# The bonus term of the first twelve attention cells as two-column matmuls, and another order of the first operations

## The chip, the cores and the metric

The kernel runs on one core of a Trainium2 chip. The metric is the device time of one execution in microseconds, the median of several executions. A core has five engines that run their own instruction streams: PE (TensorE, matmul; PEld is its loading of weights), DVE (VectorE), ACT (ScalarE), POOL (GpSimd) and SP (SyncE, which here issues nearly all DMA transfers).

## The reference

Three layers follow one another: a linear attention with a decaying state and a bonus `u` for the present token, a mixture of 4 experts that is computed densely, and an MLP with `h * cos(h)`.

```python
# attention: batch 4, heads 8, sequence 768, head size 48
for t in range(S):
    kt, vt, rt = (k[:, :, t], v[:, :, t], r[:, :, t])
    cur = np.einsum('bhd,bhe->bhde', u[None] * kt, vt)
    y[:, :, t] = np.einsum('bhd,bhde->bhe', rt, state + cur)
    state = w[None, :, :, None] * state + np.einsum('bhd,bhe->bhde', kt, vt)
# experts: N = 3072 tokens, D = 384, E = 4, F = 1024
for e in range(E):
    h = np.maximum(x @ w1[e], 0.0)
    out += p[:, e:e + 1] * (h @ w2[e])
# MLP: 384 -> 2048 -> 384
h = x @ w_in
out = (h * np.cos(h)) @ w_out
```

The bonus of a token is one number per head, `sum over d of r*u*k`, times the value row `v` of that token.

## The kernel before

**Attention** is cut into 24 cells `c`, each of 128 tokens (two chunks of 64) of one batch element with all 8 heads in 4 pairs. The first four cells begin the four batch elements. A cell loads `t` (tile `rkt`: r and k with channels in the partitions, heads in pairs) and `tok` (tile `tok`: r, k, v with tokens in the partitions). Its steps, in the names that the order tables show:

- `a_r` and `a_kt` scale r and k in `rkt` by powers of the decay (128x512 products, on DVE and POOL). The product of scaled r and scaled k at one token holds one surplus factor 1/w per channel.
- `a_ru`, `a_rk`, `a_sum`, `a_dv` make the bonus from `tok`: r times u (POOL, 128x384), times k (DVE, 128x384), a sum over d (DVE, into `dsum`), and that times v (POOL, in place in `tok[:, 0:2]`).
- `a_kp` (DVE) scales k for the state. `a_score0` and `a_state0` (later both in `a_first`) are 16 matmuls of 64x64 and 16 of 64x48, `a_mask` (DVE) masks the scores into `s`, `a_state` (ACT, DVE) and `a_state2` (three POOL products) carry the state on.
- `a_in` (16 matmuls of `s` by v) and `a_out` (8 or 16 matmuls of the state by r) sum into one PSUM bank, and the last operation of `a_out` adds the bonus and writes `yo` (DVE).
- `a_x` transposes `yo` on PE into the bank `px`; `split` writes a high part `xh` (ACT) and a low part `xl` (DVE), the inputs of the experts' matmuls.

Cells 0 and 1 of the kernel before have the bonus in another way: `l_ru` (ACT, 4 small products a cell) makes r times u, `l_bonus_pe` makes a second set of 16 score matmuls of it, `l_mask(c, 1)` keeps their diagonal (DVE), and a second run of `a_in` adds them.

**Experts and MLP** are a list of items. An item is 9 matmuls up (`hp`) and 9 down (`a`), each with weights of 128x128 and 512 moving columns (256 in the first items), in fp32r with high and low parts: three products for each pair. Weight blocks arrive by DMA in tile `s` and `w_split` makes high and low parts of them (`w`: ACT, then DVE or POOL).

**Order.** Every engine runs its instructions in the order of the program, which is written by hand. The first operations stand line by line in the last part of the function: set-up, cells 0 and 1, and `a_r`, `a_kt` for cell 2. Then the loop over items begins. A table `offsets` gives each step of cell c a place `6 * c + offset`; sorted by it, the steps are dealt out between the matmuls of the items (`mix`), the PE steps so many per item, the others as they come. SP issues DMA in program order too; a transfer waits there for its buffer and for an earlier transfer of the same slot.

Of the kernel before, what the change touches and what calls it, by code (L numbers as in the profile page):

```python
# [26 lines left out]
def attention_moe_cos_mlp_kernel(  # L27
# [61 lines left out]

    HD = HP * D  # L90
    ONE_GROUP = 4
    mask = at_p.tile([128, 2, C], F32, name="mask")
    wk_tok = at_p.tile([128, 2, HP, D], F32, name="wk_tok")
    u_tok = at_p.tile([128, 2, HP, D], F32, name="u_tok")
    pw = at_p.tile([128, HP, 129], F32, name="pw")
# [3 lines left out]
    sw = [at_p.tile([128, HP, D], F32, name=f"sw{b}") for b in range(B)]  # L99

    kps = [at_p.tile([128, 2 * HD + 16], F32, name=f"kp{x}") for x in range(2)]
    cells = [(b, i) for i in range(NCH) for b in range(B)]
    yd = {}
    pair_ps = ps_p.tile([128, 2, 512], F32, name="pair_ps")
# [103 lines left out]
                    )  # L208


    def l_load(c):
        b, i = cells[c]
        t = ld_p.tile([128, 8, HP, D], F32, tag="tok", name="tok")
        nc.sync.dma_start(out=t[:, 2:8].rearrange("q x p d -> q (x p d)"), in_=tok_in[b, i][:, 2 * HD:])
        ld[c]["tok"] = t

    def l_ru(c, ps):
        if "ru" not in ld[c]:
            ld[c]["ru"] = acc[2].rearrange("q b d -> q (b d)")[:, c * 512:c * 512 + 512].rearrange("q (p t) -> q p t", p=HP)
        for p in ps:  # L220
            nc.scalar.activation(out=ld[c]["ru"][:, p, :], in_=ld[c]["t"][:, 0, p, :], func=ACTF.Copy, scale=wpair[:, 1, p:p + 1])

    def l_bonus_pe(c):
        a_score_pe(c, False, ld[c]["ru"], ld[c]["ps_s"])

    def l_mask(c, x):
        ps = ld[c]["ps_s" if x else "ps"]
        s_ = t_p.tile([128, 2, HP, C], F32, tag="s", name="s")
        nc.vector.tensor_tensor(
            out=s_.rearrange("q c p t -> q c (p t)").rearrange("q c (p t) -> q c p t", t=C),  # L230
            in0=ps[:, :, HD:HD + HP * C].rearrange("q c (p t) -> q c p t", t=C),
            in1=mask[:, x].unsqueeze(1).unsqueeze(1).to_broadcast([128, 2, HP, C]),
            op=ALU.mult,
        )
        ld[c]["s"] = s_
# [32 lines left out]
    def a_mask(c):  # L268
        ps = ld[c]["ps"]
        s_ = t_p.tile([128, 2, HP, C], F32, tag="s", name="s")  # L270
        nc.vector.tensor_tensor(
            out=s_.rearrange("q c p t -> q c (p t)").rearrange("q c (p t) -> q c p t", t=C),
            in0=ps[:, :, HD:HD + HP * C].rearrange("q c (p t) -> q c p t", t=C),
            in1=mask[:, 0].unsqueeze(1).unsqueeze(1).to_broadcast([128, 2, HP, C]),
            op=ALU.mult,
        )
        ld[c]["s"] = s_
# [28 lines left out]
    def a_out(c):  # L306
        b, i = cells[c]
        d = ld[c]
        tok, t, ps = d["tok"], d["t"], d["ps_y"]
        apart = c >= ONE_GROUP  # L310
        if apart:
            a_in(c)
        for p in range(HP):
            for ch in range(2):
                if i == 0 and ch == 0:
                    continue
                for par in range(2):
# [11 lines left out]
        y4, p4 = yo.rearrange("q (p a d) -> q a p d", a=2, d=D), ps[:, :, 0:HD].rearrange("q a (p d) -> q a p d", d=D)  # L329
        if "ru" in d:  # L330
            nc.scalar.activation(out=y4, in_=p4, func=ACTF.Copy)
        else:
            nc.vector.tensor_tensor(out=y4, in0=p4, in1=tok[:, 0:2], op=ALU.add)
# [12 lines left out]

    def a_x(c):
        b, i = cells[c]
        if i < PASS_TB:
            px = x_bank()[:, 0:DM].rearrange("q (k t) -> q k t", k=KD)  # L350
            for kk in range(KD):
                nc.tensor.transpose(px[:, kk, :], ld[c]["yo"][:, kk * 128:kk * 128 + 128], ident)
            split(xh[i][:, :, b * 128:b * 128 + 128], xl[i][:, :, b * 128:b * 128 + 128], px)
        ld.pop(c)
# [10 lines left out]
    def a_one(c):  # L365
# [3 lines left out]
            a_first(c)  # L369

    offsets = [
        (a_load_t, -15), (a_load_tok, -15.5), (a_ru, -9), (a_r, -5.6), (a_rk, -5.5), (a_kt, -4), (a_kp, -2.6), (a_sum, -2.5), (a_dv, -2.4),
        (a_one, 0), (a_in, 2.4), (a_out, 3), (a_state2, 3.2),
    ]
    on_pe = (a_one, a_in, a_out, a_x)
    steps = sorted((6 * c + o, c, k_) for c in range(NC_ + 1) for k_, (f, o) in enumerate(offsets) if (c < NC_ or f == a_one) and not (f == a_in and c >= ONE_GROUP))
    ahead = {(f, c) for f, _ in offsets for c in range(2)}
    ahead |= {(f, 2) for f in (a_load_t, a_load_tok, a_r, a_ru, a_kt)} | {(a_load_t, 3), (a_load_tok, 3)}
    steps = [(offsets[k_][0], c) for key, c, k_ in steps if (offsets[k_][0], c) not in ahead]


# [238 lines left out]
    def warm(n):  # L620
# [3 lines left out]
        for _ in range(n):  # L624
            nc.tensor.matmul(hp, wu_a, wu_b, start=True, stop=True)

    wpair = at_p.tile([128, 3, HP], F32, name="wpair")
    tk = at_p.tile([128, HP, 2, C], F32, name="tk")

    def setup():  # L630
        nc.sync.dma_start(out=wpair[:, 0:2].rearrange("q a p -> q (a p)"), in_=w_pair)
        a_load_t(0)
        l_load(0)
        a_load_t(1)
        prob_load()
# [9 lines left out]
        for x, op in enumerate((ALU.is_gt, ALU.is_equal)):  # L645
            for o in (0, 64):
                nc.gpsimd.affine_select(
                    out=mask[o:o + 64, x], in_=mask[o:o + 64, x], pattern=[[1, C]], base=0, channel_multiplier=-1,
                    compare_op=op, fill=0.0,
                )  # L650


    def powers():
# [15 lines left out]
        nc.gpsimd.tensor_tensor(out=uw, in0=uw, in1=wp, op=ALU.mult)  # L669
        n = 1  # L670
        while n < 96:
            k_ = min(n, 96 - n)
# [104 lines left out]
    with tc.manual_schedule():  # L777
# [2 lines left out]
        setup()  # L780
        warm(14)
        powers()
        w_loads(1)
        a_load_t(2)
        nc.sync.dma_start(out=u_tok.rearrange("q a p d -> q (a p d)"), in_=u_rep)
        a_load_tok(2)
        w_loads(3)
        a_r(0)
        a_kt(0, nc.vector)
        l_ru(0, (0, 1))  # L790
        table()
        l_ru(0, (2, 3))
        a_score0(0)
        a_kp(0)
        a_state0(0)
        a_kt(1)
        l_mask(0, 0)
        l_bonus_pe(0)
        a_in(0, True, False)
        l_mask(0, 1)  # L800
# [11 lines left out]
        a_load_t(3)
        a_load_tok(3)
        w_loads(4)
        a_in(1, True, False)
        l_mask(1, 1)
        a_x(0)
        a_state(1)
        a_in(1, False)
        prob_norm()  # L820
        prob_store()
        warm(1)
        a_out(1)
        a_state2(0)
        a_r(2)
        a_kt(2)
        a_ru(2)
        w_splits(2)
# [309 lines left out]
```

## Time and profile before

| | |
|---|---|
| median of 3 executions | 1284.65 us (1284.12 to 1285.16) |
| profiled execution | 1283.49 us |
| its span, first to last instruction | 1281.4 us |
| PE busy | 1263.5 us (99%) |
| DVE, ACT, POOL busy | 758.7, 472.8, 219.4 us |
| mean granted clock of PE | 0.995 |
| PE busy in the first 22.20 us | 16.02 us |

The busy time of PE counts overlapping matmuls once, and says little on how dense they are. That is read from the starts of successive matmuls. A line of the timeline holds start, length, engine, source line, operation, output <- inputs, shape, count, and in brackets the idle time before it with what ended it. "issue" means that nothing in the trace explains the wait.

### The profile page before, as it was taken

The numbers are of one execution on the slowest core, as the hardware profiler recorded it, in microseconds if no ns is written. First come the engines' busy times: TensorE is split into PE (matmuls) and PEld (weight loads), VectorE is DVE, ScalarE is ACT, GpSimd is POOL, SyncE is SP. The second block draws the span as 40 slices with busy tenths as digits, with TensorE's granted clock in tenths as the row PEclk, the third lists the DMA queues.
The fourth block names the chain that finished last, engine by engine and source line by source line (L and its number), as shares of the span: only waits on it lengthen the run. The fifth ranks groups of instructions, "written<-read, shape, count | busy, mean of one in ns | idle before, by whom it ended". The sixth has DMA issues, their size and how long they took to land.

```text
span 1281.4 us, 20582 instructions
## 1 busy us (share of the span) xinstructions
PE 1263.5 (99%) x8516; PEld 1046.3 (82%) x8517; DVE 758.7 (59%) x1255; ACT 472.8 (37%) x826; POOL 219.4 (17%) x235
## 2 busy tenths in 40 slices
PE   7999999999999999999999999999999999999997
PEld 5888888888888888888888888888888888888886
DVE  6785675433233366556546557534777777777775
ACT  3221221121122222122122112114777777777774
POOL 5764554111111111000111111112001001001000
PEclk8999999999999999999999999999999999999999
DMA  7552464121013235234234134224005006006001
GB/s 277 186 209 89 174 225 151 40 70 34 21 58 119 74 119 169 75 103 144 60 112 149 58 96 130 62 109 153 2 17 181 25 27 198 23 1 188 18 18 51
DMA packets 54247, 128.72 MB, mean 100 GB/s; under 512 B 5025, under 2 KB 27522, under 8 KB 54146
## 3 DMA queue, kind: packets, MB, share of 16 engines
q1 hardware_dynamic: 49394, 102.03, 24.0%
q0 software_dynamic: 4608, 25.17, 6.2%
q8 instruction: 69, 1.13, 0.4%
q14 instruction: 32, 0.26, 0.1%
q10 hardware_dynamic: 144, 0.13, 0.0%
HBM read 105.24 MB, written 22.07 MB: 99 GB/s over the span
## 4 chain that ended last, share of the span: by engine, by line


## 5 line engine op out<-in xcount | busy, mean ns | idle before, releaser
L488 PE MATMUL hp<-xh,w 128*128 128x512 f32 (+1 forms) x888 | 347.4, 391 | 1.0 <-ACT xh L108 0.6
L489 PE MATMUL hp<-xl,w 128*128 128x512 f32 (+1 forms) x888 | 341.9, 385 | 1.5 <-DVE xl L109 1.5
L490 PE MATMUL hp<-xh,w 128*128 128x512 f32 (+1 forms) x888 | 341.8, 385 | 0.0
L556 PE MATMUL a<-gh,w 128*128 128x512 f32 (+1 forms) x880 | 338.4, 385 | 0.0
L558 PE MATMUL a<-gl,w 128*128 128x512 f32 (+1 forms) x880 | 337.7, 384 | 0.0
L557 PE MATMUL a<-gh,w 128*128 128x512 f32 (+1 forms) x880 | 337.7, 384 | 0.0
L497 ACT ACTIVATE gh<-hp 128x512 fp32r<-128x512 f32 (+1 forms) x200 | 116.2, 581 | 596.7 <-PE hp L490 583.7
L498 DVE SCALAR_TENSOR_TENSOR gl<-hp,gh 128x512 fp32r<-128x512 f32 (+1 forms) x200 | 133.1, 667 | 305.9 <-ACT gh L497 305.1
L488 PEld LDWEIGHTS hp<-xh,w 128*128 128x128 f32 x888 | 167.7, 189 | 35.2 <-ACT xh L108 0.8
L489 PEld LDWEIGHTS hp<-xl,w 128*128 128x128 f32 x888 | 167.9, 189 | 32.9 <-DVE xl L109 1.7
L490 PEld LDWEIGHTS hp<-xh,w 128*128 128x128 f32 x888 | 167.6, 189 | 33.1
L556 PEld LDWEIGHTS a<-gh,w 128*128 128x128 f32 x880 | 165.5, 188 | 33.2 <-ACT rr L515 0.4
L558 PEld LDWEIGHTS a<-gl,w 128*128 128x128 f32 x880 | 165.4, 188 | 32.6
L557 PEld LDWEIGHTS a<-gh,w 128*128 128x128 f32 x880 | 165.5, 188 | 32.2
L579 POOL TENSOR_TENSOR acc<-acc,pm 128x512 f32<-128x512 f32 x54 | 72.6, 1373 | 563.9 <-DVE pm L578 563.9
L517 DVE SCALAR_TENSOR_TENSOR hs<-rr,hs 128x512 f32<-128x512 f32 x96 | 67.4, 702 | 62.0 <-ACT rr L516 62.0
L509 DVE SCALAR_TENSOR_TENSOR rr<-ni,hs 128x512 f32<-128x512 int32 x96 | 66.3, 691 | 44.6 <-ACT ni L508 44.6
L515 ACT ACTIVATE rr<-rr 128x512 f32<-128x512 f32 x96 | 60.8, 633 | 86.0 <-DVE rr L510 86.0
L407 POOL DMA_DIRECT2D w<-dec x32 | 17.1, 536 | 300.3 <-PE a L558 299.5
L510 DVE SCALAR_TENSOR_TENSOR rr<-ni,rr 128x512 f32<-128x512 int32 x96 | 66.5, 693 | 3.3
L109 DVE TENSOR_TENSOR gl<-hs,gh 128x512 fp32r<-128x512 f32 x96 | 66.0, 688 | 0.7 <-ACT gh L108 0.7
L405 DVE TENSOR_TENSOR w<-s,w 128x768 fp32r<-128x768 f32 x60 | 63.6, 1059 | 1.7 <-ACT w L404 0.3
(122 smaller groups left out, 977.5 us busy)
## 6 DMA issues: line engine op xcount, KB each, us to landing
s<-in_moe_wb_dram SPq DMA_DIRECT2D x64, 384.0 KB, 3.7
w<-dec POOLq DMA_DIRECT2D x32, 768.0 KB, 4.5
tok<-in_tok_in_dram SPq DMA_DIRECT2D x22, 768.0 KB, 4.6
rkt<-in_rkt_dram SPq DMA_DIRECT2D x24, 512.0 KB, 6.1
draw<-in_moe_wb_dram SPq DMA_DIRECT2D x32, 384.0 KB, 3.8
dec<-dout SPq DMA_DIRECT2D x32, 384.0 KB, 3.0
pb<-pn SPq DMA_DIRECT2D x24, 256.0 KB, 5.0
out_dram<-acc SPq DMA_DIRECT2D x17, 256.0 KB, 2.1
```

The source lines that it names most:

```text
L488: nc.tensor.matmul(hp, wh[:, kk, :], x_h[:, kk, :], start=kk == 0, stop=False)
L489: nc.tensor.matmul(hp, wh[:, kk, :], x_l[:, kk, :], start=False, stop=False)
L490: nc.tensor.matmul(hp, wl[:, kk, :], x_h[:, kk, :], start=False, stop=kk == KD - 1)
L497: nc.scalar.activation(out=gh, in_=hp, func=ACTF.Relu)
L498: nc.vector.scalar_tensor_tensor(out=gl, in0=hp, scalar=0.0, in1=gh.bitcast(F32), op0=ALU.max, op1=ALU.subtract)
L509: nc.vector.scalar_tensor_tensor(out=rr, in0=ni, scalar=-PI2_HI, in1=hs, op0=ALU.mult, op1=ALU.add)
L510: nc.vector.scalar_tensor_tensor(out=rr, in0=ni, scalar=-PI2_LO, in1=rr, op0=ALU.mult, op1=ALU.add)
L517: nc.vector.scalar_tensor_tensor(out=hs, in0=rr, scalar=1.0, in1=hs, op0=ALU.subtract, op1=ALU.mult)
L556: nc.tensor.matmul(a, wh[:, ds], gh, start=q == 0, stop=False)
L557: nc.tensor.matmul(a, wl[:, ds], gh, start=False, stop=False)
L558: nc.tensor.matmul(a, wh[:, ds], gl, start=False, stop=q == BLK - 1)
L579: nc.gpsimd.tensor_tensor(out=o, in0=o, in1=m, op=ALU.add)
```

## The change

1. The bonus of cells 0 to 11 (`PRODS = 12`) no longer uses r of `tok`. `l_prod` (POOL) multiplies scaled r by scaled k in `rkt`, 128x512. `l_sum` sums over channels on PE: 4 matmuls, one per head pair, with the product (128x128) as weights and a moving operand of 2 columns, `uw2`, which holds u times w in the upper or lower 64 partitions. ACT copies the 8 results per token to `dsum`, and `a_dv` and the addition in `a_out` go on as before. `l_sum` writes to the bank `px`, which the transposes of `a_x` also use.
2. `a_ru`, `a_rk` and `a_sum` are gone for cells 2 to 11, and `l_ru`, `l_bonus_pe`, the second `l_mask` and the second half of `a_in` for cells 0 and 1. `l_load` leaves r out of `tok` for cells 2 to 11 as well (576 KB in place of 768 KB).
3. For cells 2 to 11 `l_sum` and `a_dv` stand at the head of `a_out`; before, `a_sum` and `a_dv` stood ahead of `a_first`. `a_kt` moves from offset -4 to -6.5.
4. The first operations stand in another order: the expert probabilities are loaded and normalised earlier, `a_out(0)` stands ahead of `a_state0(1)`, the transposes of both cells stand behind `a_out(1)`, `a_x(1)` goes to another bank, and `a_load_t(3)`, `l_load(3)` wait for `a_out(0)` as before, which comes earlier.

```diff
+    PRODS = 12
+    prods = [
+        acc[2].rearrange("q b d -> q (b d)")[:, x * 512:x * 512 + 512].rearrange("q (p t) -> q p t", p=HP) for x in range(2)
+    ]
...
+    def l_prod(c, eng=None):
+        o = prods[c % 2]
+        t = ld[c]["t"]
+        (eng or nc.gpsimd).tensor_tensor(out=o, in0=t[:, 0], in1=t[:, 1], op=ALU.mult)
+        ld[c]["prod"] = o
+
+    def l_sum(c):
+        ps = x_bank()[:, 0:2 * HP].rearrange("q (p a) -> q p a", a=2)
+        for p in range(HP):
+            nc.tensor.matmul(ps[:, p, :], ld[c]["prod"][:, p, :], uw2[:, p, :], start=p == 0, stop=True, skip_group_check=True)
+        ds = t_p.tile([128, 2, HP], F32, tag="dsum", name="dsum")
+        nc.scalar.activation(out=ds.rearrange("q a p -> q p a"), in_=ps, func=ACTF.Copy)
+        ld[c]["ds"] = ds
...
         apart = c >= ONE_GROUP
+        if 2 <= c < PRODS:
+            l_sum(c)
+            a_dv(c)
         if apart:
             a_in(c)
...
-            px = x_bank()[:, 0:DM].rearrange("q (k t) -> q k t", k=KD)
+            px = (pair_ps[:, 0] if c == 1 else x_bank())[:, 0:DM].rearrange("q (k t) -> q k t", k=KD)
...
     offsets = [
-        (a_load_t, -15), (a_load_tok, -15.5), (a_ru, -9), (a_r, -5.6), (a_rk, -5.5), (a_kt, -4), (a_kp, -2.6), (a_sum, -2.5), (a_dv, -2.4),
+        (a_load_t, -15), (l_load, -15.5), (a_load_tok, -15.5), (a_ru, -9), (a_kt, -6.5), (a_r, -5.6), (l_prod, -5.55), (a_rk, -5.5), (a_kp, -2.6), (a_sum, -2.5), (a_dv, -2.4),
         (a_one, 0), (a_in, 2.4), (a_out, 3), (a_state2, 3.2),
     ]
...
+        prob_norm()
         w_loads(1)
         a_load_t(2)
+        l_load(2)
+        w_loads(3)
         nc.sync.dma_start(out=u_tok.rearrange("q a p d -> q (a p d)"), in_=u_rep)
-        a_load_tok(2)
-        w_loads(3)
         a_r(0)
         a_kt(0, nc.vector)
-        l_ru(0, (0, 1))
+        prob_scale()
+        prob_store()
         table()
-        l_ru(0, (2, 3))
+        l_prod(0)
+        a_kt(1)
         a_score0(0)
         a_kp(0)
+        a_mask(0)
         a_state0(0)
...
```

The program's order on PE at its start, before: behind the set-up transposes (`px<-ident,tk`), cell 0 and cell 1 up to the first item's matmul (`hp`). `L203` are scores, `L189` the state, `L295` `a_in`, `L321` `a_out`, `L352` the transposes of `a_x`, `L625` warm-up matmuls.

```order
L203 MATMUL ds_ps<-acc_106,rkt 64x64 x16
L295 MATMUL dy_ps<-tok,s 64x48 x32
L203 MATMUL pair_ps<-rkt 64x64 x16
L189 MATMUL ds_ps<-tok,kp_128 64x48 x16
L321 MATMUL dy_ps<-st_1_112,rkt 64x48 x8
L203 MATMUL ds_ps<-acc_106,rkt 64x64 x16
L295 MATMUL dy_ps<-tok,s 64x48 x16
L352 MATMUL px<-ident,yo 128x128 x3
L295 MATMUL dy_ps<-tok,s 64x48 x16
```

The same place of the changed kernel, where `L207` are scores, `L193` the state, `L230` `l_sum`, `L293` `a_in`, `L322` `a_out`, `L354` the transposes:

```order
L230 MATMUL px<-uw_132,acc_106 128x2 x4
L293 MATMUL dy_ps<-tok,s 64x48 x16
L207 MATMUL pair_ps<-rkt 64x64 x16
L322 MATMUL dy_ps<-st_1_112,rkt 64x48 x8
L193 MATMUL ds_ps<-tok,kp_128 64x48 x16
L230 MATMUL px<-uw_132,acc_106 128x2 x4
L293 MATMUL dy_ps<-tok,s 64x48 x16
L322 MATMUL dy_ps<-st_1_115,rkt 64x48 x8
L354 MATMUL px<-ident,yo 128x128 x3
```

Two sets of 16 scores and two of 16 `a_in` matmuls are gone, two sets of 4 two-column matmuls are in, and `a_out(0)` stands ahead of the state of cell 1.

In the changed kernel PE has this at cell 4, behind the up matmuls of an item (`L490` to `L492`):

```order
L492 MATMUL hp<-xh_98,w 128x256
L230 MATMUL px<-uw_132,acc_106 128x2 x4
L293 MATMUL pair_ps<-tok,s 64x48 x16
L322 MATMUL pair_ps<-st_2_113,rkt 64x48 x2
L322 MATMUL pair_ps<-st_0_111,rkt 64x48 x2
```

The four matmuls of `l_sum` are new here; what follows them followed the up matmul `hp` directly. Cells 2 to 11 have this once each.

DVE between the end of cell 1 and the state of cell 2, before: `L109` is `xl`, `L405` a weight split, `L149` `a_rk`, `L158` `a_kp`, `L153` `a_sum`, `L137` `a_r`.

```order
L137 TENSOR_TENSOR rkt<-rkt,pw 128x512
L405 TENSOR_TENSOR w<-s,w 128x768
L109 TENSOR_TENSOR xl_101<-px,xh_98 128x3x128
L405 TENSOR_TENSOR w<-s,w 128x768
L149 TENSOR_TENSOR tok<-tok 128x384
L158 TENSOR_TENSOR kp_127<-tok,wk_tok 128x384
```

And in the changed kernel, where `L330` is the addition of the bonus into `yo`, `L141` `a_r`, `L113` `xl`, `L407` the weight split, `L162` `a_kp`:

```order
L330 TENSOR_TENSOR yo<-dy_ps,tok 128x2x4x48 x2
L141 TENSOR_TENSOR rkt<-rkt,pw 128x512
L113 TENSOR_TENSOR xl_101<-px,xh_98 128x3x128
L113 TENSOR_TENSOR xl_101<-pair_ps,xh_98 128x3x128
L407 TENSOR_TENSOR w<-s,w 128x768 x2
L162 TENSOR_TENSOR kp_127<-tok,wk_tok 128x384
```

`a_rk` is gone from this stretch, and the first weight split has moved behind the `xl` of cell 1.

## Rows read from the trace of the kernel before

**Rows 1.** Stretches: busy us (instructions) of PE, PEld, DVE, ACT, POOL; clock, DMA, GB/s:

```profile
0.00:22.20 22.20, 16.02 (x378) 10.93 (x380) 10.98 (x31) 9.64 (x25) 9.43 (x24) 0.92 0.79 286
22.20:60.00 37.80, 33.58 (x640) 30.65 (x641) 29.38 (x45) 11.17 (x26) 30.40 (x30) 0.91 0.60 201
600.00:800.00 200.00, 200.00 (x884) 165.74 (x883) 117.20 (x217) 41.07 (x65) 24.42 (x18) 1.00 0.32 100
```

**Rows 2.** Waits of PE over the whole span: us in total, times, longest:

```profile
PE ds_ps L189 <- issue: 2.9, 1, 2.9
PE pair_ps L189 <- DVE kp L158: 1.7, 1, 1.7
PE hp L489 <- DVE xl L109: 1.5, 1, 1.5
PE pair_ps L295 <- DVE st L252: 0.4, 1, 0.4
PE hp L488 <- DVE gl L498: 0.4, 1, 0.4
```

**Rows 3.** Timeline of PE and PEld around a cell's transposes and scores:

```profile
61.43 0.28 PE L489 MATMUL hp<-xl,w 128*128 128x256 f32 x1
61.44 0.19 PEld L490 LDWEIGHTS hp<-xh,w 128*128 128x128 f32 x1
61.55 0.28 PE L490 MATMUL hp<-xh,w 128*128 128x256 f32 x1
61.57 0.35 PEld L352 LDWEIGHTS px<-ident,yo 128*128 128x128 f32 x3
61.67 0.49 PE L352 MATMUL px<-ident,yo 128*128 128x128 f32 x3
...
62.09 0.69 PE L203 MATMUL pair_ps<-rkt 64*64 64x64 f32 x32
```

**Rows 4.** Timeline of PE in the first operations:

```profile
14.92 0.50 PE L189 MATMUL ds_ps<-tok,kp 64*64 64x48 f32 x20 [2.93 <-issue]
...
16.54 1.11 PE L295 MATMUL dy_ps<-tok,s 64*64 64x48 f32 x32
...
21.07 0.55 PE L352 MATMUL px<-ident,yo 128*128 128x128 f32 x3
...
26.95 1.11 PE L189 MATMUL pair_ps<-tok,kp 64*64 64x48 f32 x32 [1.74 <-DVE kp L158]
```

**Rows 5.** DMA queues from 12.0 to 12.5 us: packets, MB, share of 16 engines:

```profile
q1 hardware_dynamic: 33, 0.20, 98.0%
q8 instruction: 1, 0.02, 12.8%
```

**Rows 6.** Timeline of ACT and DVE between the transposes of cell 1 and the state of cell 2:

```profile
21.66 0.49 ACT L108 ACTIVATE xh<-px 128x384 fp32r<-128x384 f32 x1
...
22.04 0.83 ACT L404 ACTIVATE w<-s 128x768 fp32r<-128x768 f32 x1
...
23.95 1.28 DVE L405 TENSOR_TENSOR w<-s,w 128x768 fp32r<-128x768 f32 x1
...
25.16 0.86 DVE L149 TENSOR_TENSOR tok<-tok 128x384 f32<-128x384 f32 x1
...
25.94 0.95 DVE L158 TENSOR_TENSOR kp<-tok,wk_tok 128x384 f32<-128x384 f32 x1
```

**Rows 7.** Two of the stretches of 2 us, columns as in the first group:

```profile
16.00:18.00 2.00, 2.00 (x61) 1.89 (x50) 0.69 (x1) 1.22 (x2) 0.70 (x1) 0.50 0.45 113
...
30.00:32.00 2.00, 2.00 (x37) 1.71 (x36) 1.35 (x2) 1.02 (x3) 1.68 (x2) 0.50 0.59 236
32.00:34.00 2.00, 2.00 (x25) 1.81 (x24) 0.42 (x1) 1.08 (x2) 2.00 (x3) 0.74 0.22 25
```

**Rows 8.** Operations by form, over the span: busy us, mean ns, idle before:

```profile
L145 POOL TENSOR_TENSOR tok<-tok,u_tok 128x384 f32<-128x384 f32 x22 | 24.8, 1129 | 11.5 <-DMA tok<-in_tok_in_dram 11.4
L165 POOL TENSOR_TENSOR tok<-tok,dsum 128x384 f32<-128x384 f32 x22 | 18.3, 830 | 63.2 <-DVE dsum L153 63.2
```

More of the change, by code (lines that the diff above doesn't have):

```diff
@@ L91, in attention_moe_cos_mlp_kernel @@
     ONE_GROUP = 4
-    mask = at_p.tile([128, 2, C], F32, name="mask")
+    PRODS = 12
+    mask = at_p.tile([128, C], F32, name="mask")
     wk_tok = at_p.tile([128, 2, HP, D], F32, name="wk_tok")
@@ L208, in a_score_pe, with l_load @@
                     )
-    def l_load(c):
+    def l_load(c, eng=None):
         b, i = cells[c]
@@ L214, in l_load @@
         nc.sync.dma_start(out=t[:, 2:8].rearrange("q x p d -> q (x p d)"), in_=tok_in[b, i][:, 2 * HD:])
[L215 to L235, printed above, removed]
+        ld.setdefault(c, {})["tok"] = t
+    def l_prod(c, eng=None):
[10 more added lines that the diff above has]
+        ld[c]["ds"] = ds
     def a_state(c):
@@ L273, in a_mask @@
             in0=ps[:, :, HD:HD + HP * C].rearrange("q c (p t) -> q c p t", t=C),
-            in1=mask[:, 0].unsqueeze(1).unsqueeze(1).to_broadcast([128, 2, HP, C]),
+            in1=mask.unsqueeze(1).unsqueeze(1).to_broadcast([128, 2, HP, C]),
             op=ALU.mult,
@@ L328, in a_out @@
         d["yo"] = yo
[L329 to L333, printed above, removed]
+        nc.vector.tensor_tensor(
+            out=yo.rearrange("q (p a d) -> q a p d", a=2, d=D),
+            in0=ps[:, :, 0:HD].rearrange("q a (p d) -> q a p d", d=D),
+            in1=tok[:, 0:2],
+            op=ALU.add,
+        )
         if apart:
@@ L375, in attention_moe_cos_mlp_kernel @@
     on_pe = (a_one, a_in, a_out, a_x)
-    steps = sorted((6 * c + o, c, k_) for c in range(NC_ + 1) for k_, (f, o) in enumerate(offsets) if (c < NC_ or f == a_one) and not (f == a_in and c >= ONE_GROUP))
+    steps = sorted((6 * c + o, c, k_) for c in range(NC_ + 1) for k_, (f, o) in enumerate(offsets) if (c < NC_ or f == a_one) and not (f == a_in and c >= ONE_GROUP) and not (f in ((a_load_tok, a_ru, a_rk, a_sum, a_dv) if c < PRODS else (l_load, l_prod))))
     ahead = {(f, c) for f, _ in offsets for c in range(2)}
-    ahead |= {(f, 2) for f in (a_load_t, a_load_tok, a_r, a_ru, a_kt)} | {(a_load_t, 3), (a_load_tok, 3)}
+    ahead |= {(f, 2) for f in (a_load_t, l_load, a_r, l_prod, a_kt)} | {(a_load_t, 3), (l_load, 3)}
     steps = [(offsets[k_][0], c) for key, c, k_ in steps if (offsets[k_][0], c) not in ahead]
@@ L625, in warm @@
             nc.tensor.matmul(hp, wu_a, wu_b, start=True, stop=True)
+    uw2 = at_p.tile([128, HP, 2], F32, name="uw2")
     wpair = at_p.tile([128, 3, HP], F32, name="wpair")
@@ L631, in setup @@
         nc.sync.dma_start(out=wpair[:, 0:2].rearrange("q a p -> q (a p)"), in_=w_pair)
+        prob_load()
         a_load_t(0)
@@ L634, in setup @@
         a_load_t(1)
-        prob_load()
         l_load(1)
@@ L638, in setup @@
             nc.vector.memset(t[:, 2 * HD:], 0.0)
+        nc.gpsimd.memset(uw2, 0.0)
         nc.gpsimd.memset(ident, 1.0)
@@ L644, in setup @@
         nc.gpsimd.memset(mask, 1.0)
[L645 to L650, printed above, removed]
+        for o in (0, 64):
+            nc.gpsimd.affine_select(
+                out=mask[o:o + 64], in_=mask[o:o + 64], pattern=[[1, C]], base=0, channel_multiplier=-1,
+                compare_op=ALU.is_gt, fill=0.0,
+            )
     def powers():
@@ L668, in powers @@
             n *= 2
-        nc.gpsimd.tensor_tensor(out=uw, in0=uw, in1=wp, op=ALU.mult)
+        for a in range(2):
+            x = slice(64 * a, 64 * a + 64)
+            nc.gpsimd.tensor_tensor(out=uw2[x, :, a], in0=uw[x], in1=wp[x], op=ALU.mult)
         n = 1
@@ L699, in prob_norm, with prob_scale @@
         nc.vector.tensor_scalar(out=p_s, in0=p_s, scalar1=1e-9, scalar2=None, op0=ALU.add)
+    def prob_scale():
         nc.vector.reciprocal(out=p_s, in_=p_s)
@@ L782, in attention_moe_cos_mlp_kernel @@
         powers()
+        prob_norm()
         w_loads(1)
         a_load_t(2)
+        l_load(2)
+        w_loads(3)
         nc.sync.dma_start(out=u_tok.rearrange("q a p d -> q (a p d)"), in_=u_rep)
-        a_load_tok(2)
-        w_loads(3)
         a_r(0)
         a_kt(0, nc.vector)
-        l_ru(0, (0, 1))
+        prob_scale()
+        prob_store()
         table()
-        l_ru(0, (2, 3))
+        l_prod(0)
+        a_kt(1)
         a_score0(0)
         a_kp(0)
+        a_mask(0)
         a_state0(0)
[L796 to L800, printed above, removed]
         a_state(0)
+        l_sum(0)
+        a_in(0)
         a_r(1)
-        a_in(0, False)
+        l_prod(1)
+        a_dv(0)
         a_score0(1)
         a_kp(1)
-        l_ru(1, (0, 1, 2, 3))
+        a_mask(1)
+        a_out(0)
         a_state0(1)
-        a_out(0)
-        l_mask(1, 0)
-        l_bonus_pe(1)
-        w_splits(1, nc.gpsimd)
[L812 to L816, printed above, removed]
-        a_x(0)
[L818 to L828, printed above, removed]
+        a_state(1)
+        l_sum(1)
+        a_dv(1)
+        a_load_t(3)
+        l_load(3)
+        w_loads(4)
+        a_in(1)
+        w_splits(1, nc.gpsimd)
+        a_out(1)
+        a_r(2)
+        a_x(0)
         warm(2)
         a_x(1)
+        w_splits(2)
+        a_kt(2)
+        l_prod(2)
+        a_state2(0)
         a_state2(1)
```

## The prediction, made before the changed kernel ran

> **What bounds the kernel now.** I read the stretches first: after about 60 us PE is busy all the time, and DVE and POOL are not (in 600 to 800 us DVE has 117 of 200 us) [rows 1]. The loss of PE lies at the start: 6.2 of the first 22.2 us and 4.2 of the next 37.8 us are idle. Next the waits of PE, in which only one is long without a named cause, 2.9 us for "issue" in the state matmuls of cell 1, then 1.7 us for `kp` of cell 2 and 1.5 us for `xl` [rows 2]. From 28 us on PE waits for little more than two times 0.4 us [rows 2]. So the rule for this kernel: whatever the change adds to PE behind the start is paid in full, whatever it takes from DVE, POOL or DMA there is worth at most those few tenths, and everything that the start can give back must come from the time up to the state matmuls of cell 2 at 26.95 us [rows 4]. From there PE runs without a break.
>
> **What is added to PE.** `l_sum` is 4 matmuls, for cells 2 to 11 in the stretch that is bound by PE. The kernel has no fp32 matmul of this shape, so its price comes from neighbours. An fp32 matmul that is no transpose shows as two loads and two matmuls: a cell's 16 scores are x32 [rows 3]. So `l_sum` is 8 pairs, each a load of 128 columns of weights and a matmul of 2 columns. The nearest row is the transposes of `a_x`, also 128x128 in fp32. There the first load starts at 61.57 and its matmul at 61.67; three loads last 0.35 us together with about 0.14 for one, so (0.35 - 0.14) / 2 = 0.105 us from one load to the next [rows 3]. The three matmuls are (0.49 - 0.28) / 2 = 0.105 us apart, if the last one lasts 0.28 us like its neighbours. Is that the 128 columns of the load or the 128 columns of the matmul? The experts' rows say that it is the load: the next load (61.44) starts with the matmul before it (61.43), and its own matmul follows at 61.55, 0.11 us after, though that matmul has twice the columns [rows 3]. Then 2 moving columns do not shorten a pair: 8 x 0.107 = 0.86 us a cell. The step to 64x64 tiles behind it is paid already, since `a_in` or `a_out` followed a 128x128 matmul before too. For 10 cells: **+8.6 us**. The lower bound is the pitch of 64x64 pairs, 0.69 us for 32 less about 0.22 for the last, 0.015 us a pair [rows 3]: 80 x 0.015 = 1.2 us. The upper bound is a load that is not overlapped at all, 0.14 us: 11.2 us. I take 8.6, since the transposes have the same load.
>
> **What is taken from DVE and POOL.** For each of the ten cells DVE loses `a_rk` (0.86 us at cell 2 [rows 6]) and `a_sum`; POOL trades a product of 128x384, 1.13 us [rows 8], for one of 128x512. ACT gains a small copy. Since PE does not wait for them after 60 us, this is worth nothing there. Before 60 us it may remove the two waits of 0.4 us [rows 2] or part of them: **-0.5 us**, with 0 and -1 as bounds.
>
> **The start.** The wait of 2.9 us ends at 14.92 [rows 4]. In it the instruction queue moves one packet, at 12.0 to 12.5 us, while data hold 98% of the DMA engines [rows 5]. I read this as PE out of instructions, with the next block late behind data. The amount of instructions that PE has run until then decides where it hits. Counted off the order, PE has at that place two score sets of 64 instructions, one state set, a bonus set, an `a_in` set and more behind it; the changed kernel gets there about a quarter through `a_in(1)`, a good part of a cell later in the program. The block is asked for a fixed number of instructions earlier; there the new `l_sum(0)` of 0.9 us stands in front, so the request comes some 0.9 us later, and with the same load on DMA the wait ends at about 15.8 us. Behind it the old kernel still had 20 state pairs, `a_out(0)`, a bonus set, two sets of `a_in` for cell 1, and came to the transposes of cell 1 at 21.07 [rows 4], 6.15 us later. The new one has three quarters of one `a_in` set, `a_out(1)`, 3 transposes and two warm-up matmuls. At the upper clock, with 0.69 us for a set of 32 pairs and 0.49 for 3 transposes [rows 3], and the warm-up taken like the transposes, that is 0.5 + 0.3 + 0.45 + 0.45 = 1.7 us. At the lower one, where a set of `a_in` takes 1.11 us [rows 4] and where PE stood at 16 to 18 us [rows 7], it is about 3.0. So the transposes of cell 1 start at 17.5 to 18.8 in place of 21.07: 2.3 to 3.6 us earlier. From the transposes to the state of cell 2 the chain stays as long. It loses `a_rk`, 0.86 us, but the first weight split on DVE, which ran ahead of `xl` before, now stands behind it, so that `xh` 0.49, a weight copy on ACT 0.83, two splits of 1.28 or more, and `kp` 0.95 follow one another [rows 6]: 0.6 + 0.5 + 0.8 + 1.3 + 1.3 + 0.95 = 5.5, against 26.95 - 21.07 = 5.9. The start gives back **-2.9 us**, bounds -1.6 (block later still, since the transfers of cell 3 now start during the wait) and -6.5 (no wait).
>
> The Trainium skill speaks against that wait: "Runtime: NRT & Kernel Launch", section "Instruction fetch mechanics", has the sequencer fetch the next block while it runs the present one, and calls the cost mostly hidden. By the page nothing would stall; if the changed kernel followed it, the sum would be some 3 us lower, +1.7. The trace of the kernel before has the 2.9 us [rows 2], so I keep the wait.
>
> **The clock.** After the thin work up to 26 us PE stands at the lower clock: 0.50 at 30 to 32 us and 0.74 at 32 to 34 [rows 7]; a microsecond of dense work there costs half a microsecond. The changed kernel has the same thin stretch, earlier. The dense work begins with the low clock in both; I take **-0.5 us**, and 2.5 either way as bounds. The removed DMA (0.2 MB a cell, 2 MB in all) is hidden by PE in both: nothing.
>
> **The sum.** +8.6 - 0.5 - 2.9 - 0.5 = +4.7 us. The profiled execution took 1283.49 us for a span of 1281.4; with the sum it would be 1288.2. It lies 1.16 us under the median of the runs, 1284.65, and I put the sum on the median: **1289.3 us**, slower by 0.37%. A difference under 0.2%, 2.6 us, can hardly be told from none here.
>
> **Rivals.**
>
> *The start gives back as much as the sums cost (same).* If the block of instructions is there in time, up to 3 us more are won. If the continuous work then begins at the upper clock, 2.5 us are won besides. 8.6 - 5.9 - 2.5 - 0.5 = -0.3: 1284.4 us. For it: the block may come in time at 98% DMA load by a little luck, since the packet is moved 0.5 us after PE stopped [rows 4, 5]. Against it: the changed kernel issues the same transfers in the same first microseconds. By the page on instruction fetch this is how it would go.
>
> *A two-column matmul costs by its columns (faster).* If weight loads of successive pairs lie beside one another, as those of the 64x64 pairs do at 0.015 us [rows 3], a group of 8 costs 0.12 us and ten cost 1.2: 1284.65 + 1.2 - 3.9 = 1282.0 us. It becomes faster than before by more than can be told from no change if a group costs under 0.13 us. For it: the 64x64 pairs. Against it: those lie in four different quarters of the array, and the transposes, which fill it, do not do that. The Trainium skill, "TensorE: Matmul & The Clock Gate", section "Back-to-back issue gap", gives matmuls of 1 to 64 columns about 60 cycles from one to the next, 25 ns; as an estimate from that page ten groups would cost 2.0 us. The transposes' 0.105 us from load to load [rows 3] speaks for the weights as the limit.
>
> *The sum of the bonus comes late (slower still).* `a_dv` used to be ready before the cell began. Now it stands behind `l_sum`, ACT's copy and POOL's queue, with 0.83 us of its own [rows 8], and DVE's addition waits for it with `kp` and the low parts of the next item queued behind. POOL is busy for 30.4 of 37.8 us up to 60 us [rows 1]. If cells 2 to 5 each hold PE up by 0.7 us, 2.8 us are added: 1292.1 us. Against it: DVE has `a_rk`, 0.86 us [rows 6], and a reduction less to do per cell, and the transposes that need `yo` come some 2 us behind the end of `a_out`.
>
> **Chances.** The forecast 0.62, same by the start 0.18, cheap sums 0.09, late bonus 0.11. The forecast's own range, 1286.2 to 1291.5, lies for a small part within 0.2% of before. So faster 0.08, same 0.23, slower 0.69. The range of 8 in 10 is 1284.0 to 1292.6.
>
> **What the new profile would show.** `l_sum` rows of 8 pairs, about 0.11 us apart, each group 0.8 to 0.9 us from the up matmul to `a_in`; at 0.02 apart the first term is wrong. A wait for "issue" in `a_in(1)`, ended at 15 to 16.5 us; if there is none, the start gives more. The first matmul of an item some 3 us before 22.2, the state of cell 2 near 24. The clock low for some 6 us of dense work. New waits of PE for `yo`, `kp` or `gl` between 24 and 60 us would mean that the bonus is late.

## The result and the profile after

The changed kernel takes 1292.33 us (median of 4 runs, 1290.79 to 1294.04) against 1284.38 us for the kernel before beside it (4 runs, 1283.71 to 1285.16): ratio 1.0066, 95% interval 1.0054 to 1.0078. It is slower by 0.66%, some 8 us; the forecast was 1289.3 with a sum of +4.7, its own range ended at 1291.5 and the range of 8 in 10 at 1292.6. The profiled execution took 1293.16 us for a span of 1291.4, which is 10.0 us over the profiled span before.

The stretches of the changed kernel, with the columns of [rows 1] and [rows 7]:

```profile
0.00:22.20 22.20, 17.99 (x269) 13.31 (x269) 12.62 (x32) 7.12 (x17) 13.37 (x26) 0.75 0.76 286
...
600.00:800.00 200.00, 200.00 (x884) 165.64 (x884) 116.42 (x217) 41.89 (x68) 21.79 (x17) 1.00 0.34 106
10.00:12.00 2.00, 2.00 (x70) 1.98 (x71) 1.14 (x2) 0.80 (x4) 1.31 (x2) 0.81 1.03 419
...
30.00:32.00 2.00, 2.00 (x12) 2.00 (x12) 0.05 (x1) 0.63 (x3) 2.00 (x2) 0.57 0.20 78
...
94.00:96.00 2.00, 1.09 (x50) 0.95 (x50) 0.00 (x0) 0.19 (x1) 1.83 (x2) 1.00 0.37 142
96.00:98.00 2.00, 2.00 (x24) 1.66 (x25) 1.30 (x3) 0.00 (x0) 1.84 (x5) 0.64 0.02 6
98.00:100.00 2.00, 2.00 (x9) 1.71 (x8) 0.38 (x1) 0.60 (x1) 1.41 (x1) 0.51 0.91 252
```

The long stretch from 600 us on is as it was in [rows 1], so the loss lies ahead of it. Up to 22.2 us PE is busy 2 us longer than in [rows 1], though it has 109 instructions fewer: the granted clock of that stretch fell from 0.92 to 0.75. The 0.81 of 10 to 12 us puts the fall at 11.2 us, and the 0.57 of 30 to 32 us puts the rise at 31.7. And there is a second piece of low clock, in 96 to 100 us, behind 2 us in which PE was busy for only 1.09.

The waits of PE over the span, as in [rows 2]:

```profile
PE pair_ps L193 <- DVE kp L162: 2.0, 1, 2.0
PE pair_ps L322 <- issue: 1.7, 2, 0.9
...
PE ds_ps L193 <- DVE kp L162: 1.3, 1, 1.3
```

The 2.9 us for "issue" in the start are gone. In their place are two waits of the same kind in `a_out` of later cells, where the kernel before had none.

PE's timeline of the changed kernel, at the start, at a cell's `l_sum`, and around the second of these waits:

```profile
13.95 1.87 PE L230 MATMUL px<-uw,acc 128*128 128x2 f32 x8
...
19.72 0.85 PE L354 MATMUL pair_ps<-ident,yo 128*128 128x128 f32 x3
...
25.57 1.10 PE L193 MATMUL pair_ps<-tok,kp 64*64 64x48 f32 x32 [1.97 <-DVE kp L162]
...
57.99 0.28 PE L492 MATMUL hp<-xh,w 128*128 128x256 f32 x1
58.11 0.95 PE L230 MATMUL px<-uw,acc 128*128 128x2 f32 x8
58.99 0.68 PE L293 MATMUL pair_ps<-tok,s 64*64 64x48 f32 x32
...
95.97 0.55 PE L322 MATMUL pair_ps<-st,rkt 48*64 48x48 f32 x20 [0.91 <-issue]
...
96.96 0.63 PE L491 MATMUL hp<-xl,w 128*128 128x512 f32 x1
97.39 0.63 PE L492 MATMUL hp<-xh,w 128*128 128x512 f32 x1
...
100.56 0.40 PE L490 MATMUL hp<-xh,w 128*128 128x512 f32 x1
100.80 0.40 PE L491 MATMUL hp<-xl,w 128*128 128x512 f32 x1
```

The same place of a cell in the kernel before:

```profile
65.30 0.28 PE L490 MATMUL hp<-xh,w 128*128 128x256 f32 x1
65.51 0.68 PE L295 MATMUL pair_ps<-tok,s 64*64 64x48 f32 x32
```

Three readings. From the last up matmul to `a_in` it is 58.99 - 57.99 = 1.00 us now and was 65.51 - 65.30 = 0.21: a group costs **0.79 us**, and its pairs are (0.95 - 0.25) / 7 = 0.10 us apart on average, with 0.25 for a last one. Between 96.96 and 97.39 the 512-column matmuls follow each other at 0.43 us, four microseconds later at 0.24: that is the lower of the two levels, 1.2 GHz. The clock shares of 96 to 100 us, 0.64 and 0.51, make it 3.4 us (96.6 to 100.0), which at half rate costs 1.7. The last point is the state of cell 2, which marks the end of the start: 25.57 in place of 26.95 [rows 4].

**The budget of the profiled executions.** Start: -1.4 us. From the state of cell 2 to the end of the span it was 1281.4 - 26.95 = 1254.45 us and is 1291.4 - 25.57 = 1265.83: +11.4. In it are ten groups at 0.79 (7.9), two waits for instructions (1.7) and the low clock at 96.6 (1.7), together 11.3. Since the kernel before had two waits of 0.4 us there that are gone, some 0.9 us stay without a place.

The DMA queues of the changed kernel from 93.5 to 94.0 us, as in [rows 5]:

```profile
q1 hardware_dynamic: 87, 0.18, 99.7%
q8 instruction: 1, 0.02, 11.6%
```

The wait that ends at 95.97 has the pattern of [rows 5]: one instruction packet while data hold nearly all of the DMA engines, and PE goes on some 2 us later. The first wait, which ended at 69.36, has its packet at 67.0 to 67.5 us, beside data at 97.7%. That full DMA engines make such a wait is not shown by this; the runs below speak against it.

### The profile page after: what moved, and what is told of

It is laid out like the page before. It is cut to its first block, busy times and chain, and to the rows that moved or that the text cites. A ratio compares the mean times of both kernels' runs of the same rounds, so it can differ in the third digit from the quotient of the medians.

```text
span 1291.4 us, 20510 instructions
## 1 busy us (share of the span) xinstructions
PE 1275.1 (99%) x8484; PEld 1059.5 (82%) x8484; DVE 745.5 (58%) x1235; ACT 471.9 (37%) x828; POOL 222.2 (17%) x239
## 4 chain that ended last, share of the span: by engine, by line
## 5 line engine op out<-in xcount | busy, mean ns | idle before, releaser
L490 PE MATMUL hp<-xh,w 128*128 128x512 f32 (+1 forms) x888 | 347.5, 391 | 0.6 <-ACT xh L112 0.6
L492 PE MATMUL hp<-xh,w 128*128 128x512 f32 (+1 forms) x888 | 342.0, 385 | 0.0
L490 PEld LDWEIGHTS hp<-xh,w 128*128 128x128 f32 x888 | 167.8, 189 | 34.6 <-ACT xh L112 1.0
L492 PEld LDWEIGHTS hp<-xh,w 128*128 128x128 f32 x888 | 168.1, 189 | 33.3
L113 DVE TENSOR_TENSOR gl<-hs,gh 128x512 fp32r<-128x512 f32 x96 | 66.0, 688 | 0.7 <-ACT gh L112 0.7
L407 DVE TENSOR_TENSOR w<-s,w 128x768 fp32r<-128x768 f32 x60 | 64.4, 1074 | 1.8 <-ACT w L406 0.5
```

The source lines that it names most:

```text
L490: nc.tensor.matmul(hp, wh[:, kk, :], x_h[:, kk, :], start=kk == 0, stop=False)
L492: nc.tensor.matmul(hp, wl[:, kk, :], x_h[:, kk, :], start=False, stop=kk == KD - 1)
```

## The experiments

The theory after this reading: the ten groups cost about 8 us in full, the new start gives back 1.5 to 3, and the waits for instructions and the low clock in the cells belong to the changed order and take the rest. The rival: the groups themselves are cheaper, and the new start or the order of its DMAs makes the cells slower. Under both lies the question of what makes a pair cost 0.1 us. The interval behind each ratio is 95%; the median of the kernel before, measured beside each run, stands in brackets.

### The new start without the sums, and the sums without the new start

The first keeps the new first operations and the sums of cells 0 and 1, and gives cells 2 to 11 the bonus of before (`PRODS`, the loads and the steps, with `a_kt` back at offset -4). The second is the kernel before with `l_prod` and `l_sum` in cells 2 to 11 alone, and the loads and offsets that go with them. The cut shows the first.

```diff
-    PRODS = 12
+    PRODS = 2
...
-        l_load(2)
+        a_load_tok(2)
...
-        l_load(3)
+        a_load_tok(3)
...
-        l_prod(2)
+        a_ru(2)
```

> The new first operations with sums on PE in cells 0 and 1 alone; cells 2 to 11 make their bonus in the old way. Theory A (the ten groups of two-column matmuls in cells 2 to 11 cost some 0.8 us each, the start gives back what the trace shows, 1.4 us): 1283 us, 1 to 2 below before. Rival B (the new start costs, by its longer low clock of PE): 1288 to 1292 us. Rival C (the start gives back the 2.9 us of the prediction, and something else in the cells eats it): 1281.5 us.

> The old first operations, with the product on POOL and the two-column matmuls in cells 2 to 11. Theory A: before plus 8 us for the groups, plus 0 to 3 for waits for instructions and a low clock in the cells: 1292 to 1295 us. Rival B (the start costs, the groups are cheap): 1284 to 1287 us.

Start alone: 1282.04 us (1281.62 to 1285.47, 11 runs) [1284.02], ratio 0.9987 (0.9978 to 0.9996): the start gives 2.0 us, between theory A and rival C, and rival B is out. Sums alone: 1292.99 (1291.71 to 1295.28, 5 runs) [1284.02], ratio 1.0074 (1.0061 to 1.0088), +9.0, as theory A has it. Together +7.0, against 7.9 measured for the whole change; they add up within the intervals. So the sums cost their time with the old start too, and the rival falls. The profile of the sums alone has 1.9 us of waits for instructions in the cells and the low clock from 97.3 to 100.7 us. The profile of the start alone has no low clock behind 31 us, but it has a wait for instructions in a cell as well, and the DMA queues at its packet, from 72.5 to 73.0 us, are nearly empty of data:

```profile
75.06 0.38 PE L490 MATMUL hp<-xh,w 128*128 128x256 f32 x1 [1.25 <-issue]
```

```profile
q1 hardware_dynamic: 17, 0.02, 13.2%
q8 instruction: 1, 0.02, 11.6%
```

So either part of the change brings such waits into cells that had none before; of these two profiles only that with the sums has the low clock there. And a wait for instructions does not need full DMA engines: here PE went on some 2 us after the packet just the same. The execution that was profiled here took 1284.58 us, 2.5 over the median of its kernel; its clock fell at 10.9 us and its state of cell 2 came at 27.27, later than before. It stands for a slow start of this kernel, and the 2.0 us are read from the medians.

### The sums twice

```diff
-        for p in range(HP):
-            nc.tensor.matmul(ps[:, p, :], ld[c]["prod"][:, p, :], uw2[:, p, :], ...)
+        for x in range(2 if c > 1 else 1):
+            for p in range(HP):
+                nc.tensor.matmul(ps[:, p, :], ld[c]["prod"][:, p, :], uw2[:, p, :], ...)
```

> The changed kernel, but the four two-column matmuls run twice in a row in cells 2 to 11; this leaves a wrong bonus there. Theory A (each of the 8 pairs waits for its load of 128 columns): 80 pairs more at about 0.11 us: +8.6 us on the changed kernel, 1301 us. Rival (a pair costs by its 2 columns): +1 to 2 us, 1294 us. If pairs bring waits for instructions with them, more than 9 us.

1302.87 us (1299.15 to 1303.73, 4 runs) [1284.02], ratio 1.0144 (1.0128 to 1.0159), +18.9, and 10.5 over the changed kernel. Timeline of PE at one cell:

```profile
53.97 0.28 PE L493 MATMUL hp<-xh,w 128*128 128x256 f32 x1
54.09 1.84 PE L231 MATMUL px<-uw,acc 128*128 128x2 f32 x16
55.87 0.68 PE L294 MATMUL pair_ps<-tok,s 64*64 64x48 f32 x32
```

Four stretches of 4 us, with the columns of [rows 1]:

```profile
34.00:38.00 4.00, 4.00 (x64) 3.67 (x66) 1.43 (x4) 1.60 (x3) 3.84 (x5) 0.57 0.71 211
82.00:86.00 4.00, 4.00 (x25) 3.83 (x28) 2.06 (x4) 0.38 (x1) 3.07 (x4) 0.58 0.58 173
102.00:106.00 4.00, 4.00 (x40) 3.37 (x33) 1.77 (x4) 0.60 (x1) 3.64 (x5) 0.57 0.44 127
116.00:120.00 4.00, 4.00 (x12) 3.11 (x11) 2.35 (x4) 0.60 (x1) 3.76 (x5) 0.57 0.62 195
```

All the waits of PE behind 33 us in this run:

```profile
PE pair_ps L615 <- DVE xl L113: 0.3, 1, 0.3
PE px L355 <- ACT gh L500: 0.2, 1, 0.2
```

The second eight pairs cost 55.87 - 53.97 - 1.00 = 0.90 us a cell, 9.0 in all: theory A holds, and the rival by columns is out. Beside them stands the clock: four falls to the lower level inside the cells, 3.4 us each, with PE marked busy throughout, three more than in the profile of the changed kernel. No wait for instructions is left behind 33 us, against the last sentence of the expectation. At 1.7 us a fall this does not add up: 9.0 + 5.1, less the two waits of 1.7 that are gone, is 12.4, but behind the state of cell 2 (24.33 here) the two profiles differ by 10.4. So the falls cost less here, or 2 us were won elsewhere. A fall needs no wait of PE ahead of it, then, and the two surprises of the changed kernel can occur apart. The DMA queues of this run from 69.0 to 69.5 us show the other side of that, a packet of instructions beside full engines and no wait behind it:

```profile
q1 hardware_dynamic: 71, 0.19, 95.0%
q8 instruction: 1, 0.02, 11.2%
```

### What a pair costs: bf16, fewer pairs, operands swapped

bf16: products and `uw2` are bf16 tiles, so four pairs in place of eight. One pair: a single matmul with all 8 columns in place of the four with 2, in cells 2 to 11. Swapped: the 2 columns of `uw2` are the weights, the product's 128 columns move.

```diff
-    prods = [acc[2]...[:, x * 512:x * 512 + 512]... for x in range(2)]
+    prods = [at_p.tile([128, HP, 128], mybir.dt.bfloat16, name=f"prod{x}") for x in range(2)]
...
-    uw2 = at_p.tile([128, HP, 2], F32, name="uw2")
+    uw2 = at_p.tile([128, HP, 2], mybir.dt.bfloat16, name="uw2")
```

```diff
+        if c > 1:
+            nc.tensor.matmul(ps.rearrange("q p a -> q (p a)"), ld[c]["prod"][:, 0, :],
+                             uw2.rearrange("q p a -> q (p a)"), ...)
-        for p in range(HP):
+        for p in range(HP if c < 2 else 0):
```

```diff
...
+                nc.tensor.matmul(bank[0:2, p * 128:p * 128 + 128], uw2[:, p, :],
+                                 ld[c]["prod"][:, p, :], ...)
...
```

> The changed kernel with product and two-column operand in bf16: 4 loads and 4 matmuls in a cell in place of 8 and 8, at less precision. Theory A: half the pairs are gone, 4 us or more less: 1287 to 1288.5 us, and the groups last 0.4 us or less. Rival (the time is in the chain of the bonus or in the start, not in the pairs): 1291 to 1293 us.

> The changed kernel, but in cells 2 to 11 one matmul with 8 columns stands for the four with 2 columns: 2 pairs of load and matmul in place of 8. The bonus there then sums the wrong products; all other work and all waits stay. Theory A (the time goes by pairs, 0.8 to 0.86 us for 8): 60 pairs less, 6 us under the changed kernel, or a little less where a wait for the bonus comes to light: 1286 to 1287.5 us. Rival (the cost is in the chain product, sum, copy, product with v, whatever the pairs): 1290 us or more.

> The changed kernel, but in cells 2 to 11 the two operands of the sums change places: the 2 columns are the weights, the product is the moving operand with 128 columns. The sums land in 2 partitions, and what is copied from there is no bonus of these cells; the instructions and their waits are the same in number. If the load of 128 columns sets the price of a pair (step of the prediction): the load is now of 2 columns, a pair falls to what 128 fp32 columns cost to stream, which no row shows (0.053 to 0.107 us); 0 to 4 us under the changed kernel, and pairs under 0.08 us apart would speak for the load. Rival (any fp32 pair that fills the rows of the array costs 0.1 us, whichever operand has the columns): as the changed kernel.

bf16: 1285.03 us (1284.59 to 1286.29, 11 runs) [1284.02], ratio 1.0011 (1.0002 to 1.002). One pair: 1285.33 (1284.49 to 1287.02, 11 runs) [1283.71], 1.0015 (1.0006 to 1.0024). Swapped: 1291.54 (1290.84 to 1292.55, 5 runs) [1283.47], 1.0057 (1.0044 to 1.007). The first two lie with theory A and even below its ranges, by 2.0 and 0.7 us; the third lies with the rival. PE's timeline with bf16 at a cell:

```profile
50.03 0.28 PE L490 MATMUL hp<-xh,w 128*128 128x256 f32 x1
50.15 0.25 PE L228 MATMUL px<-uw,prod 128*128 128x2 bf16 x4
50.33 0.68 PE L291 MATMUL pair_ps<-tok,s 64*64 64x48 f32 x32
```

The longest waits of PE with bf16 behind 30 us:

```profile
PE px L352 <- DVE yo L336: 1.1, 2, 0.6
PE pair_ps L320 <- issue: 1.1, 1, 1.1
PE a L557 <- issue: 0.8, 1, 0.8
PE px L352 <- DVE yo L328: 0.7, 2, 0.5
```

And PE's timeline with swapped operands:

```profile
57.79 0.28 PE L499 MATMUL hp<-xh,w 128*128 128x256 f32 x1
58.00 1.03 PE L231 MATMUL px<-acc,uw 128*2 128x128 f32 x8
58.97 0.68 PE L300 MATMUL pair_ps<-tok,s 64*64 64x48 f32 x32
```

With 2 columns of weights and 128 moving, pairs are (1.03 - 0.27) / 7 = 0.109 us apart, with 0.27 for the last: the same price. A whole group is even dearer, 58.97 - 57.79 - 0.21 = 0.97 us in place of 0.79. So an fp32 pair with 128 columns on either side costs about 0.1 us here, and the slimmer weights saved nothing. Whether the 128 columns set that price, or any fp32 pair over all 128 rows costs it, as the rival has it, is not shown: no run has such pairs in a row that are thin on both sides. In bf16, with the same columns, four pairs take 0.25 us together, and a whole group costs 50.33 - 50.03 - 0.21 = 0.09 us in place of 0.79. A group of one fp32 matmul, two pairs, costs 0.13 by the same difference.

The budget of bf16 closes nearly as well. From the state of cell 2 (25.07) to the end is 1258.2 us, 3.8 over the kernel before. Ten groups are 0.9; the waits shown, 3.7, less the 0.8 that went, are 2.9. But its clock rose at 29.0 us (0.75 in 28 to 30 us), 2 us nearer to the state of cell 2 than before, which gives 1.1 back; so about 1 us stays without a place here too. The waits for `yo` were 0.2 us before: with short groups PE comes to the transposes before the bonus sum is added. In the changed kernel PE's own 0.79 us hid most of that, and the waits for `yo` there are 0.3 us, 0.8 in its second profile. None of the three forms has the low clock in the cells, which theory A did not count. bf16 and swapped still have 1.9 us of waits for instructions there, and one pair has 1.1.

### The changed kernel once more

> The changed kernel once more, unaltered, for its time beside the run above and for a second profile. If the waits for instructions and the low clock inside the cells belong to the groups, the second profile has them too, 1 to 4 us together; if they were chance of one execution, the part behind the state of cell 2 is shorter by up to 3 us. Time: 1291 to 1293.5 us.

1291.93 us (1290.3 to 1294.87, 6 runs) [1283.47], ratio 1.0062 (1.005 to 1.0074), within the forecast. Its profile is a second execution of the same program. PE's timeline in the start:

```profile
15.51 0.56 PE L293 MATMUL dy_ps<-tok,s 64*64 64x48 f32 x22 [1.09 <-issue]
...
18.05 0.85 PE L354 MATMUL pair_ps<-ident,yo 128*128 128x128 f32 x3
...
24.13 1.10 PE L193 MATMUL pair_ps<-tok,kp 64*64 64x48 f32 x32 [1.80 <-DVE kp L162]
```

Stretches of 2 us of this second profile, with the columns of [rows 1]:

```profile
16.00:18.00 2.00, 1.60 (x25) 1.20 (x22) 0.83 (x2) 1.37 (x3) 0.89 (x1) 0.87 0.93 376
...
26.00:28.00 2.00, 2.00 (x39) 1.77 (x38) 1.23 (x2) 1.65 (x4) 1.92 (x3) 0.57 0.89 344
...
70.00:72.00 2.00, 2.00 (x11) 1.83 (x10) 1.23 (x2) 0.00 (x0) 0.39 (x1) 0.50 0.93 311
96.00:98.00 2.00, 2.00 (x7) 1.63 (x6) 1.67 (x3) 0.00 (x0) 1.84 (x4) 0.50 0.32 49
```

Here the clock stays high until 17.5 us, the wait for instructions in `a_in(1)` exists and ends at 15.51, the transposes of cell 1 start at 18.05 and the state of cell 2 at 24.13: these three as forecast. In the first profile the clock fell at 11.2 us, so that `l_sum(1)` took 1.87 us in place of 1.05, no wait for instructions followed, and the state of cell 2 came at 25.57. The start is worth 1.4 us in the one and 2.8 in the other. What the second execution won there it paid in the cells, where it has the low clock twice, at 68.7 to 72.1 and 96.0 to 99.4 us, and waits for instructions of 2.0 us. Together that is 5.4 us, more than the 1 to 4 expected.

### Can the start give more?

All three are made from the start alone. The first moves the normalising of the probabilities behind `a_kp(1)`, since the `kp` of cell 0, for which PE waited 1.3 us, stands behind 1.27 us of it on DVE. The second sets `warm(5)` into PE's gap ahead of the state of cell 0. The third has both.

```diff
-        prob_norm()
...
-        prob_scale()
-        prob_store()
...
         a_kp(1)
+        prob_norm()
         a_mask(1)
+        prob_scale()
+        prob_store()
```

```diff
         a_mask(0)
+        warm(5)
         a_state0(0)
```

> The new first operations alone (as in the run of the start alone), but the probabilities are normalised behind the scaling of k of cell 1 on DVE, no longer ahead of that of cell 0. Theory D (the start gave back less than forecast since this work of DVE holds up the state of cell 0 by some 0.8 us): 0.5 to 0.9 us under the start alone, 1281.2 to 1281.6 us. Rival E (it is the clock that PE has from 11 to 17 us on, which does not depend on this): within 0.3 us of the start alone.

> The start alone, with 5 warm-up matmuls more in the idle time of PE ahead of the state of cell 0. Rival E (the idle time at 7 to 9 us lets the clock fall at about 11 us; with it the first cells run at half rate): the clock falls some 4 us later or not at all before the wait for cell 2, and the time is 1 to 2 us under the start alone, 1280 to 1281 us. Theory D: no gain, or 0.3 us more since the warm-up stands ahead of the state.

> Both edits on the start alone. If D and E each hold in part: 1280 to 1281 us. If neither: 1282 us.

Late probabilities: 1282.65 us (1281.05 to 1283.76, 11 runs) [1283.71], ratio 0.9991 (0.9982 to 1.0). Warm-up in the gap: 1282.73 (1281.99 to 1284.23, 11 runs) [1283.71], 0.9992 (0.9983 to 1.0001). Both: 1283.48 (1282.74 to 1286.5, 11 runs) [1283.71], 1.0001 (0.9992 to 1.001). None is better than the start alone. Theory D's gain did not come, though PE's wait for the `kp` of cell 0 fell from 1.3 to 0.8 us; rival E's later fall of the clock came, but not its time; and with both edits the time is above even the 1282 of neither. Since the profiled execution of the start alone was a slow one, its early fall at 10.9 us does not stand for its median, and a later fall may have been there already. DVE's timeline of the first shows why the wait did not fall further:

```profile
8.26 0.75 DVE L162 TENSOR_TENSOR kp<-tok,wk_tok 128x384 f32<-128x384 f32 x1 [1.06 <-ACT wk_tok L689]
```

`kp` now waits for ACT's `wk_tok`; the probabilities had filled that time. The clock of these three fell at 17.0, 17.4 and 15.6 us, and the third has a fall at 73.6 to 77.0 behind a wait for instructions of 1.6 us, without any group of sums in that cell. The other two have one such wait in a cell each, of 1.0 us.

## Why the prediction was off, by its own steps

**What bounds the kernel: right.** DVE and POOL lost work in ten cells, and nothing came of it but the two waits of 0.4 us that went; the sums on PE are paid one for one.

**The price of the sums: right in kind and nearly in size.** Forecast 0.86 us a group and 8.6 in all, measured 0.79 and 7.9, with pairs 0.10 us apart as the transposes of [rows 3]. The reason given was that the load of 128 columns sets the pitch. The experts' rows did not show that: with the same loads, matmuls of 256 columns are 0.12 us apart [rows 3] and those of 512 are 0.24 (100.56 to 100.80 above), so their pitch goes by the moving columns. And the swapped form shows that 128 moving columns would have cost the same, so the transposes could not have told the two apart. The size was right by the nearest neighbour, not by the reason. The rival by which two-column matmuls are cheap is out. Its page, the Trainium skill, "TensorE: Matmul & The Clock Gate", section "Back-to-back issue gap", with 25 ns for short matmuls, fits the bf16 pairs of this case (0.25 us for four, some 0.16 of it for the last, so 0.03 apart), not the fp32 ones.

**The failed step: "From there PE runs without a break".** It holds for the kernel before, and the forecast carried it over to the changed one; so new waits for instructions and a low clock inside the cells were put at nothing without a reason. Measured are 1.7 to 2.0 us of waits for instructions, in two of the ten cells, and 1.7 us for each fall to the lower level, one in one profile and two in the other: 3.4 to 5.4 us where the forecast had none. That is as much as the miss, 7.95 - 4.65 = 3.3 us, or more; the sums were 0.7 cheaper, and some of the rest varies from execution to execution. The two small terms beside it were sound: for the -0.5 of removed waits 0.8 us went, and for the -0.5 of the clock at the head of the dense work the low clock behind the state of cell 2 lasted 6.1 us as before in one profile (25.57 to 31.7, against 26.95 to 33.0) and 3.6 us in the other (24.13 to 27.7), 0 to -1.2 us.

**The start: right way, a little too large.** Forecast -2.9, measured -2.0 by the start alone, in which the wait in a cell that the new start brings is paid already. The forecast chain was found row by row in one profile (-2.8) and not in the other (-1.4). When the clock fell at 11 us, the work ahead of the wait took longer, and the wait was gone; but PE lost more by the clock than by the wait. The rival by which the absent wait gives the whole cost back had the wait right for that profile and the result wrong. The page that it leaned on, the Trainium skill, "Runtime: NRT & Kernel Launch", section "Instruction fetch mechanics", calls the fetch mostly hidden. For most packets these traces agree: the instruction queue q8 moves 69 in each of the two kernels, and one wait of PE for "issue" over 0.3 us stands beside them before, two or three after. For these few it is not hidden, with 2.9 us before and 1.7 to 2.0 us in the cells after. That the block came late "behind data", as the prediction reads [rows 5], is not shown: a wait stood behind a packet beside 13.2% of data, and none behind one beside 95.0%.

**The late bonus** cost little in the changed kernel (0.3 and 0.8 us for `yo` in its two profiles, 0.2 before). With bf16 groups, which hide less of it, it costs 1.8 us. This rival's 1292.1 us, so near to the measured time, is luck: its mechanism has 2.8 us there.

**What stays open.** Low clock in the cells was seen in the profiles whose groups have eight or more fp32 pairs of 128 columns of weights and 2 moving ones: one fall in the changed kernel, two in its second profile, one with the sums alone, four with the sums twice; none with bf16, with one pair, with swapped operands or in the kernel before. That points to the thin groups, and the sums twice show that no wait is needed for it. But one start variant has a fall without groups, behind a wait, so both may do it; no run separates thin work from waits in the changed kernel itself. Nor is it known what places the waits for instructions: they come with the sums and with the new start alike, at several times and lengths in every trace but those of the kernel before and of the sums twice, and full DMA engines at the packet neither make nor are needed for one.

## What to carry to other kernels

Where an engine never waits, price each instruction added to it by the pitch of its nearest neighbour in type and width, on both of its operands, and count relief of other engines only against waits that have a row. Then ask of thin work what it does to the clock, and of changed code whether new waits for instructions come with it: both were worth more here than the 0.7 us of error in the price itself. A change of two parts is best run as its parts: the new first operations alone take 1282.04 us, ratio 0.9987 (0.9978 to 0.9996), and so beat both kernels, the one before by little more than the noise.

## What the runs showed of the hardware

In a row, an fp32 matmul of 128 columns by 2 costs two pairs at 0.10 to 0.11 us, whichever operand has the 128; the bf16 matmul of the same shape is one pair, and four of them take 0.25 us. The granted clock can fall to 1.2 GHz for 3.4 us with PE marked busy all through, as four times in the sums twice. Two executions of one program differ in when the first fall comes, at 11.2 or 17.5 us, with the state of cell 2 at 25.57 and 24.13. And where PE waited for instructions, it went on some 2 us behind their packet, with data at 99.7% of the DMA engines (95.97 us in the changed kernel) as at 13.2% (75.06 us in the start alone).
